# A gated mix of window attention and a feed-forward block, forward and backward: paired puts, first loads on two queues, a gate gradient summed on VectorE

## The chip, the cores and the metric

The kernel runs on one core of one Trainium2 chip. The metric is the device time of one execution in microseconds (us), lower being better, as the median of several executions. The engines are TensorE (PE, matmuls), VectorE (DVE), ScalarE (ACT), GpSimd (POOL) and SyncE (SP). DMAs are issued here from SP, ACT and POOL; an issue takes a place in the instruction stream of its engine, which is worked through in order.

## The reference

A gate mixes two branches over 2048 tokens of width 512, and the kernel returns the output together with the gradients of seven inputs.

```python
g = sigmoid((x * gate_w).sum(-1, keepdims=True))
# branch a: 32 heads of 16, causal, a window of 256 tokens
q, k, v = split(x @ wqkv);  p = softmax(mask(q k^T / 4));  a = (p v) @ wo
# branch b: gated ReGLU with 1376 hidden columns
gate = x @ W_gate;  up = x @ W_up;  gate = gate * (gate > 0);  b = (gate * up) @ W_down
# x is A_x in both branches
out = g * a + (1 - g) * b
out, vjp = jax.vjp(f, A_x, A_wqkv, A_wo, B_W_gate, B_W_up, B_W_down, gate_w);  grads = vjp(grad_out)
```

All arrays are bf16. The outputs are `out` and the gradients of `A_x`, `wqkv`, `wo`, the three feed-forward weights and `gate_w`.

## The kernel before

**An order that a planner writes.** The program is one long list of operations. Each has the engines that it may run on with an estimated cost in ns, the buffers it reads and writes, and a rank. `Flow.run` plays this list through with its own clock: whenever an engine is free, the ready operation of lowest rank is put on it, and its instructions are issued in that order. The order on each engine is thus fixed when the program is built. Costs of DMA issues are numbers in the calls (`ns=340` for a put, 430 or 1300 by default). `SEEDS` adds a small random part to the ranks of dense matmuls, 200 operations to a seed, so that another set of seeds gives another order. Where PE has nothing ready for long, the planner puts in a filling matmul.

**Buffers.** The on-chip arena is divided into rings, each with a number of places; an operation that opens a buffer waits, in the plan and on the chip, until the place is free. `KVT`, `QDT`, `KVr`, `K1r` and `dd` hold a stage's inputs, `R`, `OB`, `dkv` its results.

**The start.** `load_first` loads the first two halves of the x rows, the weights of the first head group, and the rows of the output's gradient, all from SP. The gate weights are loaded from POOL, once as a column (`gw_col`, spread over 128 columns as `gw_rep` by VectorE) and once for all partitions (`gw_b`). `rows_to_T` turns x and the gradient on PE, `proj` makes q, k, v and the gradient of the attention's result, and `gates` computes the gate.

**The attention.** 32 stages (8 groups of 4 heads, 4 blocks of 512 tokens) each run six units of scores from the queries' side (A) and six from the keys' side (N). Row products make scores (`L1003`), ScalarE takes the exponential (`L1045`), POOL masks (`L1021`), VectorE multiplies (`L1051`), and column products sum up (`L1071`). Between these, PE takes dense work: projections, the feed-forward block in 11 chunks (`front`, `back`), and weight gradients (`L672`, `L1354`). `load_stage` loads a stage's k, v, q from DRAM (`L950`, `L951`) and once more turned (`L952`, into `KVr`). `put` writes a stage's dq and O to `HD_d` in four pieces of 16 rows (`L933`), and `tasks_N` writes dk and dv (`L1155`). `dw` loads `HD_d` turned for the weight gradients (`L1257`), and `load_heads` loads it straight for the last part (`L1332`).

**The end.** `final` and `whole` make the output and the gradient of x, one tile of 128 tokens each. Each tile also gives one `dz` for every token. The gradient of `gate_w` is the sum over all tokens of dz times x: `gate_sum` makes it with one matmul for each of the 16 tiles (`L1421`), three tiles late, into one bank `dg`.

Of the kernel before, what the change touches and what calls it, by code (L numbers as in the profile page):

```python
# [30 lines left out]
def place(segs, dist):  # L31
# [21 lines left out]
    10644, 40677, 50928, 50391, 47256, 5130, 14352, 52294, 4187, 17826, 20428, 23758, 43565, 50024, 2925, 886,  # L53
    42283, 15231, 13752, 30525, 39203, 9215, 6352, 38931, 53278, 7326, 50008, 50973,
# [341 lines left out]
def kernel(  # L396
# [45 lines left out]
    HQ, OUTS, GLAG = (SP, ACTE), 2, 3  # L442
# [25 lines left out]
    nc.scalar.preload_act_table_set("natural_log_exp_and_others")  # L468
# [36 lines left out]
    nc.gpsimd.dma_start(gw_col[:], gate_w.rearrange("(c p) -> p c", p=P))  # L505
    nc.gpsimd.dma_start(gw_b[:], gate_w.partition_broadcast(P))
    nc.vector.tensor_copy(gw_rep[:], bc(gw_col[:], P))
# [24 lines left out]
    ring("QDT", 5, [P, W])  # L532
# [3 lines left out]
    ring("KVr", 4, [P, 4, P])  # L536
# [8 lines left out]
    ring("R", 3, [P, 4, P])  # L545
    ring("OB", 2, [P, W])
    ring("dkv", 3, [P, W])
# [16 lines left out]
    ring("rg", 4, [P, W])  # L564
# [30 lines left out]
    place_at["next"] = A0 + KB  # L595
    ring("wo4", 1, [P, DC, D], after=["QDT"])
    assert place_at["next"] <= rings["dd"].lo
    ring("wT3", 1, [P, 3 * DC, D], at=B0, after=["RW"])
    ring("RW3", 1, [P, NT, 4 * P], at=rings["dd"].lo, after=att)
# [5 lines left out]
    for nm, k in (("b_t", 3), ("x_t", 3), ("xs", 2)):  # L605
        ring(nm, k, [P, D], F32, after=att)
# [3 lines left out]
    ring("dz", 4, [P, 4], F32, after=att)  # L610
# [29 lines left out]
    def dma(fn, r=(), w=(), nbytes=0, rank=3, turn=False, deps=(), order=(), on=(SP,), ns=0, row=0):  # L640
        return op({e: 1000 if e == POOL else ns or (1300 if turn else 430) for e in on}, (lambda e: fn(EN[e])) if fn.__code__.co_argcount > len(fn.__defaults__ or ()) else (lambda e: fn()), r=r, w=w, 
                  nbytes=nbytes * (0.785 + 106 / (row or (256 if turn else 1024))), rank=rank,
                  deps=deps, order=order)
# [33 lines left out]
    by_pool = (POOL,)  # L677

    def load_proj(c):
        w3 = buf("w3")  # L680
        for w in range(3):
            dma(lambda q, w=w: q.dma_start(
                w3[:, :, w, :], A_wqkv[:, w * D + c * P:w * D + (c + 1) * P].rearrange("(c p) n -> p c n", p=P)),
                w=[(w3, w)], nbytes=128 * KB, rank=3, row=256, on=by_pool if c == 1 else (SP,))
# [4 lines left out]
    def load_ffn(fc):  # L689
        fs, f0 = fsz(fc), fc * P  # L690
        wg, wu, wdT = buf("wg"), buf("wu"), buf("wdT")
        for t_, src in ((wg, B_W_gate), (wu, B_W_up)):
            dma(lambda q, t_=t_, src=src: q.dma_start(t_[:, :, :fs], src[:, f0:f0 + fs].rearrange("(c p) f -> p c f", p=P)),
                w=[t_], nbytes=128 * KB, rank=3, row=256, on=by_pool if fc < 2 else (SP,))
# [9 lines left out]
    def load_first():  # L704
# [3 lines left out]
        def rows(dst, src_d, k):  # L708
            dma(lambda: nc.sync.dma_start(dst[:, 2 * k:2 * k + 2, :],
                                          src_d[2 * k * P:2 * (k + 1) * P, :].rearrange("(t p) d -> p t d", p=P)),  # L710
                w=[(dst, 0), (dst, ("half", k))], nbytes=256 * KB, rank=3)

        def weights(w):
            dma(lambda: nc.sync.dma_start(
                w3[:, :, w, :], A_wqkv[:, w * D:w * D + P].rearrange("(c p) n -> p c n", p=P)),
                w=[(w3, w)], nbytes=128 * KB, rank=3, row=256)
# [7 lines left out]
        dma(lambda: nc.sync.dma_start_transpose(out=woT[:], in_=A_wo[0:P, :]), w=[woT], nbytes=128 * KB, rank=3, turn=True)  # L724
        weights(0)
# [14 lines left out]
    load_first()  # L740
    for sb in range(1, NSB):
        load_rows(x_r, x_d, sb)
        load_rows(db_r, go_d, sb)
    load_ffn(0)

    def rows_to_T(dst, src, sb, rank):
        for h in range(2):
# [11 lines left out]
            for k in range(n):  # L759
# [3 lines left out]
                   r=[pt], w=[(dst, sb)], rank=1)  # L763

# [26 lines left out]
    def proj_weights(c, rank):  # L791
        w3, woT = wsets.pop(("p", c))
# [3 lines left out]
           r=[(w3, 1)], w=[(wi, 0)], rank=3)  # L796
        op({POOL: 1200}, lambda e: nc.gpsimd.tensor_copy(wi[:].rearrange("p c (h w d) -> p c w h d", w=2, d=Dh)[:, :, 1],
                                                         w3[:, :, 2, :].rearrange("p c (h d) -> p c h d", d=Dh)),
           r=[(w3, 2)], w=[(wi, 1)], rank=3)
# [741 lines left out]
```

## Time and profile before

| | |
|---|---|
| median of 3 runs | 836.26 us (834.75 to 839.38) |
| the profiled execution | 836.25 us |
| its span, first to last instruction | 834.5 us |
| mean granted TensorE clock | 0.994 |
| busy: PE, DVE, ACT, POOL | 817.0, 689.2, 603.8, 544.8 us |
| DMA moved | 152.17 MB |

The profile shows one execution. A row of a view by instructions gives the start and the time in us, the engine, the line of the kernel, the operation, the tile written and the tile read, and in square brackets how long the engine stood before and what ended that. "SPq" and "ACTq" are the queues' instruction streams, where DMA issues stand. A row by stretches gives, for every engine, the busy time and the number of instructions, then the granted clock, the share of the DMA engines and GB/s. A row by line gives counts and the least, median and greatest duration in ns.

### The profile page before, as it was taken

What the parts mean: (1) busy time and instruction counts of PE and PEld (TensorE: products, weight loads), DVE (VectorE), ACT (ScalarE), POOL (GpSimd) and SP (SyncE); (2) the same over time, 40 slices, a digit from 0 to 9 for tenths busy, and PEclk for the clock granted to TensorE, in tenths of its full rate; (3) what the DMA queues carried; (4) which work ended last, traced back from release to release, by engine and by line L of the source; (5) the groups of instructions that cost most, each with busy time, mean ns of one, the idle gap of its engine ahead of it and who ended that gap; (6) DMA issues with size and microseconds to landing.
All of it is one profiled execution on the core that took longest, in us unless ns stands there. A gap on an engine that the chain in (4) does not pass through costs nothing.

```text
span 834.5 us, 24001 instructions
## 1 busy us (share of the span) xinstructions
PE 817.0 (98%) x8717; PEld 368.9 (44%) x8717; DVE 689.2 (83%) x1264; ACT 603.8 (72%) x1223; POOL 544.8 (65%) x945
## 2 busy tenths in 40 slices
PE   8999999999999999899999989999999999999999
PEld 5533444445354445354444544343343343434444
DVE  3697899999999999799899878898899898934643
ACT  4877778788878878788888768878887887603222
POOL 5388668797697878779898445546655656401435
PEclk9999999999999999999999999999999999999999
DMA  8889647576678787889988895764686554497985
GB/s 226 224 188 204 142 117 182 109 186 166 117 200 165 160 199 170 201 208 182 227 194 182 213 218 166 185 166 115 180 192 182 160 171 126 92 308 198 280 220 173
DMA packets 317033, 152.17 MB, mean 182 GB/s; under 512 B 205233, under 2 KB 309234, under 8 KB 316274
## 3 DMA queue, kind: packets, MB, share of 16 engines
q1 hardware_dynamic: 298146, 136.22, 67.2%
q10 hardware_dynamic: 18192, 12.85, 5.2%
q0 software_dynamic: 576, 1.57, 0.8%
q8 instruction: 68, 1.11, 0.6%
q14 instruction: 51, 0.42, 0.2%
HBM read 55.02 MB, written 55.74 MB: 133 GB/s over the span
## 4 chain that ended last, share of the span: by engine, by line
PE 85%; DVE 5%; DMA 3%; POOL 2%; issue 2%; ACT 2%; SPq 1%; DVEq 0%; ACTq 0%; POOLq 0%
PE banks L672 38%; PE banks L1354 21%; PE banks L1003 14%; PE banks L1071 10%; DVE arena L1051 3%; POOL arena L1021 1%; ACT arena L1045 1%; POOL arena L878 1%; DMA ffn_d<-arena 1%; PE banks L1104 1%; PE banks L753 1%; DMA arena<-in_A_wqkv_dram 1%; DMA arena<-KV_d 1%; DMA KV_d<-arena 0%; PE banks L1421 0%
## 5 line engine op out<-in xcount | busy, mean ns | idle before, releaser
L1051 DVE TENSOR_TENSOR arena<-arena,banks 128x512 bf16<-128x512 bf16 (+2 forms) x768 | 461.8, 647 | 45.7 <-PE banks L1003 37.7
L1045 ACT ACTIVATE arena<-banks 128x512 bf16<-128x512 f32 (+2 forms) x768 | 398.7, 572 | 77.8 <-PE banks L1003 66.1
L1021 POOL TENSOR_SCALAR_AFFINE_SELECT arena<-arena 128x256 bf16<-128x256 bf16 (+1 forms) x736 | 350.0, 499 | 160.0 <-ACT arena L1045 138.7
L672 PE MATMUL banks<-arena 128*128 128x512 bf16 (+4 forms) x1984 | 394.9, 337 | 2.6 <-DMA arena<-in_A_wqkv_dram 2.1
L672 PEld LDWEIGHTS <-arena 128*128 128x128 bf16 (+1 forms) x1984 | 172.5, 99 | 156.8 <-issue 59.6
L1354 PE MATMUL banks<-arena 128*128 128x512 bf16 (+1 forms) x784 | 188.4, 381 | 1.2 <-DVE arena L1051 1.2
L1003 PE MATMUL banks<-arena 32*128 32x256 bf16 (+5 forms) x2816 | 162.4, 276 | 6.3 <-ACT arena L1045 3.0
L878 POOL TENSOR_TENSOR arena<-arena 128x512 bf16<-128x512 bf16 (+1 forms) x91 | 105.9, 1168 | 19.5 <-DVE arena L873 8.5
L1003 PEld LDWEIGHTS <-arena 16*128 16x128 bf16 (+1 forms) x2816 | 49.7, 92 | 155.4 <-issue 145.3
L650 ACT CAST arena<-banks 128x512 bf16<-128x512 f32 (+4 forms) x159 | 77.4, 497 | 50.9 <-PE banks L672 35.1
L1354 PEld LDWEIGHTS <-arena 128*128 128x128 bf16 (+1 forms) x784 | 69.2, 98 | 92.1 <-issue 21.1
L1071 PE MATMUL banks<-arena 128*32 128x384 bf16 (+5 forms) x2816 | 104.4, 278 | 3.4 <-POOL arena L1021 2.2
L1071 PEld LDWEIGHTS <-arena 128*32 128x32 bf16 (+1 forms) x2816 | 57.7, 94 | 42.0 <-issue 28.6
L1450 POOL TENSOR_TENSOR arena<-arena 128x512 bf16<-128x512 f32 x12 | 16.0, 1341 | 59.7 <-ACT arena L1449 27.9
L1100 POOL TENSOR_TENSOR arena<-arena 128x512 bf16<-128x512 f32 x32 | 37.0, 1157 | 17.5 <-issue 10.7
L1440 DVE SCALAR_TENSOR_TENSOR arena<-banks,g_all,arena 128x512 bf16<-128x512 f32 x12 | 8.9, 746 | 32.3 <-ACT arena L1449 19.7
L1449 ACT ACTIVATE arena<-banks,g_all 128x512 f32<-128x512 f32 x12 | 8.2, 687 | 32.4 <-DVE arena L1445 11.4
L878 DVE TENSOR_TENSOR arena<-arena 128x512 bf16<-128x512 bf16 (+1 forms) x41 | 28.4, 695 | 3.6 <-DMA ffn_d<-arena 3.5
L873 DVE SCALAR_TENSOR_TENSOR arena<-arena,banks 128x512 bf16<-128x512 bf16 (+1 forms) x44 | 29.8, 679 | 1.1 <-ACT arena L868 0.6
L868 ACT ACTIVATE arena<-banks 128x512 bf16<-128x512 f32 (+1 forms) x38 | 23.0, 604 | 4.2 <-PE banks L672 4.0
L652 DVE CAST arena<-banks 128x512 bf16<-128x512 f32 (+3 forms) x41 | 23.7, 589 | 2.5 <-PE banks L672 1.7
L1096 ACT ACTIVATE arena<-arena 128x512 f32<-128x512 f32 x32 | 20.2, 630 | 7.5 <-DVE arena L1095 7.4
(88 smaller groups left out, 412.6 us busy)
## 6 DMA issues: line engine op xcount, KB each, us to landing
ffn_d<-arena SPq DMA_DIRECT2D x40, 384.0 KB
arena<-ffn_d SPq DMA_DIRECT2D x88, 128.0 KB
out_dram<-arena SPq DMA_DIRECT2D x66, 128.0 KB
arena<-HD_d ACTq DMA_DIRECT2D x29, 256.0 KB
KV_d<-arena SPq DMA_DIRECT2D x32, 128.0 KB
QD_d<-arena SPq DMA_DIRECT2D x32, 128.0 KB
arena<-KV_d SPq DMA_DIRECT2D x32, 128.0 KB
arena<-QD_d SPq DMA_DIRECT2D x32, 128.0 KB
```

The lines of the kernel that those rows point to most:

```text
L650: nc.scalar.copy(out, in_)
L652: EN[e].tensor_copy(out, in_)
L672: return lambda start, stop: nc.tensor.matmul(out_fn(), lhsT=lhs_fn(), rhs=rhs_fn(), start=start, stop=stop)
L873: op({DVE: t_stt(W)}, lambda e, q=q, ups=ups: nc.vector.scalar_tensor_tensor(out=q["upm"][:fs, :], in0=q["rg"][:fs, :], scalar=0.0, in1=up ...
L878: op({POOL: t_pool(W, 2), DVE: DTT}, lambda e, q=q, k=k, a=a, b=b: EN[e].tensor_tensor(out=q["act"][:fs, k, :], in0=q[a][:fs, :], in1=q[b] ...
L1003: nc.tensor.matmul(bank, lhsT=lt[rs, ls], rhs=rt[rs, rsl], start=True, stop=True)
L1021: nc.gpsimd.affine_select(out=v.rearrange("p h (b k) -> p h b k", b=cnt), in_=v.rearrange("p h (b k) -> p h b k", b=cnt), compare_op=ALU.i ...
L1045: op({ACTE: t_act(w)}, lambda e, h=h: nc.scalar.activation(nxt.Pt[:, h, :w], nxt.S[h][:, :w], ACT.Exp), r=[nxt.S[h]], w=[(nxt.Pt, h)], rank=0)
L1051: op({DVE: t_dve(wc)}, lambda e, h=h: nc.vector.tensor_tensor(out=cur.Pd[:, h, :wc], in0=cur.Pt[:, h, :wc], in1=cur.dP[h][:, :wc], op=ALU. ...
L1071: nc.tensor.matmul(acc[32 * i:32 * i + wt.shape[1], q0:q0 + cnt * P], lhsT=wt, rhs=m[:, i % 2, col * P:(col + cnt) * P], start=(k == 0), s ...
L1100: op({POOL: t_pool(W, 2), DVE: t_dve(W)}, lambda e: EN[e].tensor_tensor(out=U[:], in0=ri[:], in1=qd[:], op=ALU.mult), r=[ri, qd], w=[U], r ...
L1354: nc.tensor.matmul(bank[:], lhsT=l_(), rhs=r_(), start=(lo + k == 0), stop=(lo + k == n - 1))
```

## The change

It has five parts.

1. dq and O are gathered for two token blocks in rings of `[P, 2, W]`, and `put` writes both at once after the odd block: 4 issues of 16 rows of 2 KB in place of 8 of 1 KB.
2. The first loads go out from SP and ACT alternately. The gate weights come in as four rows on ACT, are turned by one PE transpose and spread by VectorE; the copy for all partitions is loaded after the x rows. The activation table's load follows the DMA issues on ACT. The loads of the first feed-forward chunk and of the second head group, and the copies of the first group's weights, wait for later turns of x.
3. The gate gradient: 14 tiles are summed as dz times x in F32, the first on POOL, the others on VectorE; POOL splits the sum into two bf16 parts, and two matmuls with ones bring them into `dg`. The last two tiles are added by matmuls as before.
4. The rings `QDT`, `KVr`, `R`, `dkv`, `rg`, `b_t` and `x_t` get smaller.
5. The planner's costs of SP's issues are set anew, and there is a new set of `SEEDS`.

```diff
 SEEDS = (
-    10644, 40677, 50928, 50391, 47256, 5130, 14352, ...
+    49174, 34604, 21252, 10858, 43264, 6178, 26424, ...
-    HQ, OUTS, GLAG = (SP, ACTE), 2, 3
+    HQ, OUTS, DIRECT = (SP, ACTE), 2, 2
-    nc.scalar.preload_act_table_set("natural_log_exp_and_others")
-    nc.gpsimd.dma_start(gw_col[:], gate_w.rearrange("(c p) -> p c", p=P))
-    nc.gpsimd.dma_start(gw_b[:], gate_w.partition_broadcast(P))
-    nc.vector.tensor_copy(gw_rep[:], bc(gw_col[:], P))
-    ring("QDT", 5, [P, W])
+    ring("QDT", 3, [P, W])
-    ring("KVr", 4, [P, 4, P])
+    ring("KVr", 3, [P, 4, P])
-    ring("R", 3, [P, 4, P])
-    ring("OB", 2, [P, W])
-    ring("dkv", 3, [P, W])
+    ring("R", 2, [P, 4, P])
+    ring("OB", 2, [P, 2, W])
+    ring("dq", 2, [P, 2, W])
+    ring("dkv", 2, [P, W])
-    ring("rg", 4, [P, W])
+    ring("rg", 3, [P, W])
-    for nm, k in (("b_t", 3), ("x_t", 3), ("xs", 2)):
+    for nm, k in (("b_t", 2), ("x_t", 2), ("xs", 2), ("gx", 1)):
-        return op({e: 1000 if e == POOL else ns or (1300 if turn else 430) for e in on}, ...
+        return op({e: 1000 if e == POOL else ns or (1270 if turn else 470) for e in on}, ...
+    def load_gate():
+        dma(lambda q: q.dma_start(gw_4[:], gate_w.rearrange("(c p) -> c p", p=P)), w=[gw_in], ..., on=(ACTE,))
+        pt = buf("pro", [P, DC], BF)
+        op({PE: 60}, lambda e: nc.tensor.transpose(pt[:], gw_4[:], ident[:DC, :DC]), r=[gw_in], w=[pt], rank=0.1, mode="den")
+        def spread(e):
+            nc.vector.tensor_copy(gw_col[:], pt[:])
+            nc.vector.tensor_copy(gw_rep[:], bc(gw_col[:], P))
+        op({DVE: 500}, spread, r=[pt], w=[gw_out], rank=1)
-        rows(x_r, x_d, 0)
-        rows(x_r, x_d, 1)
-        weights(1)
-        weights(2)
-        rows(db_r, go_d, 0)
-        rows(db_r, go_d, 1)
...
-        weights(0)
+        rows(x_r, x_d, 0, SP)
+        rows(x_r, x_d, 1, ACTE)
+        weights(1, SP)
+        weights(2, ACTE)
+        weights(0, SP)
+        rows(db_r, go_d, 0, SP)
+        rows(db_r, go_d, 1, ACTE)
...
+    load_gate()
+    op({ACTE: 1300}, lambda e: nc.scalar.preload_act_table_set("natural_log_exp_and_others"), rank=4)
-    load_ffn(0)
...
+    load_ffn(0, [later[0]])
+    proj_weights(0, [later[2]])
+    load_gate_rows([later[3]])
...
     def put(src, c, half, sb, k, lane, kind):
+        if sb % 2 == 0:
+            return
         for g in range(4):
-            dma(lambda ...: nc.sync.dma_start(HD_d[c, k, r0:r0 + Dh, sb * W:(sb + 1) * W], src[lo:lo + Dh, :]),
-                r=[src], w=[(HD_d, (c, sb, kind))], nbytes=16 * KB, rank=3, ns=340)
+            dma(lambda ...: nc.sync.dma_start(HD_d[c, k, r0:r0 + Dh, (sb - 1) * W:(sb + 1) * W],
+                                              src[lo:lo + Dh].rearrange("p b s -> p (b s)")),
+                r=[src], w=[(HD_d, (c, sb - 1, kind)), (HD_d, (c, sb, kind))], nbytes=32 * KB, rank=3, ns=460, row=2048)
...
+    def gate_sum(t, dz, dz_bf):
+        done.append(t)
+        if len(done) > NT - DIRECT:
+            direct(lambda: dz_bf[:, 0:1], lambda: x_r[:, t, :], [dz_bf, x_r])
+            return
+        if len(done) == 1:
+            op({POOL: t_pool(W)}, lambda e: nc.gpsimd.tensor_scalar(gx[:], x_r[:, t, :], dz[:, 1:2], None, op0=ALU.mult), ...)
+        else:
+            op({DVE: t_stt(W)}, lambda e: nc.vector.scalar_tensor_tensor(
+                out=gx[:], in0=x_r[:, t, :], scalar=dz[:, 1:2], in1=gx[:], op0=ALU.mult, op1=ALU.add), ..., rank=4)
+        if len(done) == NT - DIRECT:
+            op({POOL: t_pool(W)}, lambda e: nc.gpsimd.tensor_copy(gx2[:, 0], gx[:]), ...)
+            op({POOL: t_pool(W, 2)}, lambda e: nc.gpsimd.tensor_tensor(out=gx2[:, 1], in0=gx[:], in1=gx2[:, 0], op=ALU.subtract), ...)
+            for k in range(2):
+                direct(lambda: ones_c[:], lambda k=k: gx2[:, k], [(gx2, k)])
```

Among the planner's costs, the turned loads of `L1257` go from 1900 to 2400 ns, those of the feed-forward activations (`L894`) from 1500 to 2000, and the loads of turned weights from 3200 to 2000 and 2200.

More of the change, by code (lines that the diff above doesn't have):

```diff
@@ L594 @@
     assert place_at["next"] <= B2, (place_at["next"], B2)
-    place_at["next"] = A0 + KB
-    ring("wo4", 1, [P, DC, D], after=["QDT"])
-    assert place_at["next"] <= rings["dd"].lo
     ring("wT3", 1, [P, 3 * DC, D], at=B0, after=["RW"])
-    ring("RW3", 1, [P, NT, 4 * P], at=rings["dd"].lo, after=att)
+    ring("wo4", 1, [P, DC, D], after=["RW"])
+    assert place_at["next"] <= B0 + 16 * KB
+    ring("RW3", 1, [P, NT, 4 * P], at=A0 + KB, after=att)
     assert place_at["next"] <= rings["PtA"].lo
@@ L763, in rows_to_T @@
                    r=[pt], w=[(dst, sb)], rank=1)
+        return turned
     def proj(c, which, sb, rank):
@@ L837, in gates @@
         accumulate(pz, [mm(lambda: pz[:], lambda c=c: gw_rep[:, c, :], lambda c=c: x_T[:, c, sl]) for c in range(DC)],
-                   [(x_T, sb)], 0.8 if sb else 1.6)
+                   [(x_T, sb), gw_out], 0.8 if sb else 1.6)
         op({ACTE: t_act(W)}, lambda e: nc.scalar.activation(ez_bc[:, sl], pz[:], ACT.Exp), r=[pz], w=[(ez_bc, sb)], rank=1)
-    proj_weights(0, 0.3)
+    wsets["pw", 0] = wsets.pop(("p", 0))
+    later = {}
     for sb in range(NSB):
-        rows_to_T(x_T, x_r, sb, 0.2)
+        later[sb] = rows_to_T(x_T, x_r, sb, 0.2)
         if sb:
@@ L1083, in tasks_A1 @@
         LO, de = (buf("acc") for _ in range(2))
-        ri, OB, U, pr, R = (buf(nm) for nm in ("ri", "OB", "U", "pr", "R"))
+        ri, U, pr, R = (buf(nm) for nm in ("ri", "U", "pr", "R"))
+        if sb % 2 == 0:
+            st["OB"] = buf("OB")
+        OB, half = st["OB"], sb % 2
         dd, qd = st["in", n][2], st["qd", n]
@@ L1114, in tasks_A2 @@
         c, half = divmod(hg, 2)
-        Da, dq = buf("acc"), buf("dkv")
+        Da = buf("acc")
+        if sb % 2 == 0:
+            st["dq"] = buf("dq")
+        dq, k = st["dq"], sb % 2
         def w2(a, i):
@@ L1158 @@
     for c in range(1, DC):
-        load_proj(c)
-        proj_weights(c, 3)
+        load_proj(c, [later[1]] if c == 1 else ())
+        proj_weights(c)
         for sb in range(NSB):
@@ L1166 @@
         if fc:
-            load_ffn(fc)
+            load_ffn(fc, [later[1]] if fc == 1 else ())
         front(fc)
@@ L1502 @@
             whole(t, late[t // 2], qks[t // 2])
-    while waiting:
-        emit_gate_sum([])
     dgs = buf("dgs", [1, D])
```

116 lines of the change are left out of this document (62 added, 54 removed).

## The prediction

> **What bounds the kernel now.** I read the page of the profile first, for the shares and the chain; then the busy time by stretches of 20 us, for where TensorE (PE) is not busy; then the chain of waits at those places, the order of time at both ends, and the DMA issues by line.
>
> ```profile
> span 834.5 us, 24001 instructions
> PE 817.0 (98%) x8717; PEld 368.9 (44%) x8717; DVE 689.2 (83%) x1264; ACT 603.8 (72%) x1223; POOL 544.8 (65%) x945
> ...
> PE 85%; DVE 5%; DMA 3%; POOL 2%; issue 2%; ACT 2%; SPq 1%; DVEq 0%; ACTq 0%; POOLq 0%
> ```
>
> PE is busy 98% of the span and carries 85% of the chain that ended last. The profiled execution took 836.25 us, 1.7 us of it outside the span, and the median of the three runs is 836.26, so I sum against 836.25. PE's work is nearly fixed, and what the change can win is PE's gaps, the two ends, and PE instructions that go away. The gaps are 834.5 - 817.0 = 17.5 us:
>
> ```profile
> core 0: us, PE busy (x) PEld busy (x) DVE busy (x) ACT busy (x) POOL busy (x), PEclk, DMA share, GB/s
> 0.00:20.00 20.00, 16.25 (x146) 10.55 (x147) 7.09 (x19) 8.45 (x17) 10.10 (x25) 0.91 0.81 226
> ...
> 60.00:80.00 20.00, 18.33 (x187) 7.18 (x184) 15.72 (x28) 14.34 (x29) 17.96 (x27) 1.00 0.90 191
> 80.00:100.00 20.00, 19.02 (x217) 8.95 (x215) 17.27 (x31) 15.71 (x31) 15.32 (x26) 1.00 0.83 174
> ...
> 340.00:360.00 20.00, 17.33 (x181) 7.23 (x179) 15.62 (x28) 14.49 (x29) 16.14 (x26) 1.00 1.06 264
> ...
> 480.00:500.00 20.00, 17.49 (x195) 8.41 (x199) 13.80 (x29) 11.84 (x24) 10.05 (x21) 0.92 0.93 211
> ...
> 540.00:560.00 20.00, 18.57 (x192) 7.37 (x190) 17.88 (x34) 15.61 (x36) 10.19 (x22) 0.91 0.73 183
> ...
> 720.00:740.00 20.00, 18.05 (x201) 7.54 (x194) 15.57 (x30) 6.70 (x16) 3.96 (x9) 1.00 0.68 199
> ...
> 800.00:820.00 20.00, 20.00 (x101) 9.52 (x100) 10.32 (x19) 4.85 (x11) 10.65 (x8) 1.00 0.92 266
> ```
>
> The first 20 us lack 3.75 us of PE. The six rows from 60 to 740 lack 1.67 + 0.98 + 2.67 + 2.51 + 1.43 + 1.95 = 11.2 us. In three of the rows the granted clock is also below 1: 0.08 and 0.09 of 20 us at 480 and 540 are 1.6 and 1.8 us more. So the start costs about 4 us, the middle about 14.6, and everything else is PE at work.
>
> **The start.** Here are both engines and the queues in order of time, then the DMA queues in the first 8.4 us:
>
> ```profile
> 0.81 1.28 ACT L468 ACT_TABLE_LOAD   x1 [0.81 <-PEq L1525]
> 0.82 0.98 SPq L709 DMA_DIRECT2D arena<-in_A_x_dram  x2
> ...
> 1.84 1.02 SPq L714 DMA_DIRECT2D arena<-in_A_wqkv_dram  x2
> ...
> 4.64 0.58 ACT L650 COPY arena<-banks 128x512 bf16<-128x512 bf16 x1 [2.54 <-PE banks L753]
> ...
> 5.50 0.83 PE L735 MATMUL banks<-ident 128*128 128x128 bf16 x12
> ...
> 6.53 0.43 DVE L507 COPY gw_rep<-gw_col 128x512 bf16<-128x512 bf16 x1 [1.45 <-DMA gw_col<-in_gate_w_dram]
> 6.88 0.75 DVE L652 COPY arena<-banks 128x512 bf16<-128x512 bf16 x2
> 8.40 3.33 PE L672 MATMUL banks<-arena 128*128 128x512 bf16 x8 [2.06 <-DMA arena<-in_A_wqkv_dram]
> 11.52 1.32 PE L672 MATMUL banks<-arena,gw_rep 128*128 128x512 bf16 x4
> ```
> ```profile
> q1 hardware_dynamic: 2212, 1.25, 52.3%
> q0 software_dynamic: 83, 0.15, 18.4%
> ```
>
> PE's first projection waits 2.06 us for wqkv. Three things stand ahead of that load. SP issues two x loads at about 0.49 us each, then two weight loads at 0.51. On the other queue, GpSimd's, the gate weights (a column gathered by single elements and a row for 128 partitions) and first weights take 18.4% of the DMA engines for 0.15 MB, against 52.3% for 1.25 MB: three times the engine time per byte. And VectorE stands 1.45 us on gw_col, with two copies of x_T queued behind it until 7.63.
>
> The change splits the issues over SP and ACT, so the second weight load leaves about two issues (1.0 us) earlier; it takes GpSimd's traffic out of this stretch and frees VectorE from gw_col. Ends: 0 and the 2.06 us of PE wait. I take 1.4, nearer the wait, since issue and traffic add up. What replaces it: the gate column arrives as four rows behind ACT's loads, and goes through one small PE transpose and a VectorE spread (0.43 us by L507). It is wanted only where the gw_rep matmuls stand (11.52), so I cost it at nothing; without that cover it costs up to the 1.45 us that VectorE waited. The table load (1.28) moves behind four ACT issues (about 2.0 us) and then ends near 4.1, ahead of ACT's first copy at 4.64: nothing. GpSimd's copies of wi and the loads of the first feed-forward chunk go later; nothing in the first 20 us reads them.
>
> The first eight projections take 3.33 us, 416 ns each, where four gw_rep matmuls take 1.32, 330 ns with their tail; the clock of the stretch is 0.91. 0.09 of 20 us is 1.8 us lost. PE had ended its twelve warming matmuls at 6.33 and then stood until 8.40. With the weights 1.4 us earlier that gap is under 0.7 us, and I expect the slow spell to go: 1.7 us, with 0 as the other end. The Trainium skill, "TensorE: Matmul & The Clock Gate", Part 1, says that the window which judges PE's activity runs freely and is not reset by a kernel's start; by that rule the spell could fall on other matmuls and the term is 0, so the sum 1.7 us higher. The rows at 480 and 540 agree that a gap brings a slow spell, while the row at 340, with a larger gap and clock 1.00, shows that it is not certain.
>
> The same skill, "DMA: Bandwidth & Descriptors", section "Issuing engines are not separate DMA queues", speaks against the two queues: all issuers end on the same engines, and a second one saves only issue time. By that rule alone the landing gain is the 1.0 us of issues and not 1.4.
>
> **Puts by pairs.** A put of dq or O leaves every second token block with 2 KB rows, so 256 issues on SP become 128.
>
> ```profile
> L933 SPq DMA_DIRECT2D HD_d<-arena x256: 315/418/1606, 75.4 to 740.8; - x128
> L1155 SPq DMA_DIRECT2D HD_d<-arena x32: 337/420/1227, 90.7 to 731.6; - x32
> ...
> L952 SPq DMA_TRANSPOSE arena<-KV_d x32: 1188/1224/1862, 18.2 to 656.2; - x32
> ```
>
> L1155 moves eight times the bytes of one L933 put with the same median, so a put of twice the bytes costs the same 0.42 us. SP loses 128 x 0.42 = 54 us out of the 665 us in which the puts lie. Everything queued on SP behind them (loads of the next stage, turned rows, activations) leaves earlier. The chain shows what that queue's lateness costs PE:
>
> ```profile
> 71.37 4.17 DMA KV_d<-arena
> ...
> 78.12 3.29 DMA ffn_d<-arena
> ...
> 339.53 3.44 DMA ffn_d<-arena
> ...
> 489.88 4.83 DMA arena<-KV_d
> ```
>
> These stand in the rows that lack 1.67, 0.98, 2.67 and 2.51 us, 7.8 in all, with 1.6 us of slow clock behind the last: 9.4 us. The new costs given to the planner for SP's issues, and the new seeds, give another order, which no row of before shows. So the ends are -9.4 (all gone) and +9.4 (as many new ones). I take a gain of a third, 3.1: SP is relieved by 54 of 665 us, which cannot remove waits on data that is really late, but shortens all of them. The put itself now comes one block later for even blocks. Its readers are the weight gradients and the head loads, which follow the attention; for the last head group the third block's rows come one stage, (734 - 30) / 32 = 22 us by the row products' ends below, later. PE works on from 734 to the tail's matmuls at 828.84 (below), some 95 us, so nothing is lost there.
>
> ```profile
> L1003 PE MATMUL banks<-arena x2816: 211/278/523, 29.7 to 734.2; 32*128 32x384 bf16 x39, 32*128 32x256 bf16 x33, 16*128 16x384 bf16 x30, 16*128 16x256 bf16 x29
> ```
>
> The rings that shrink to make room (QDT 5 to 3, KVr 4 to 3, R 3 to 2, dkv 3 to 2, rg 4 to 3, b_t and x_t 3 to 2) allow some loads only later. KVT, loaded and read beside QDT, already has three. KVr is the tight one; it is the slower rival below. I cost the rest at nothing, covered by PE's other work.
>
> **The gate's gradient.** Sixteen matmuls become four; the rest is summed on VectorE, and GpSimd splits the sum into two parts. The tail in order of time:
>
> ```profile
> 808.10 0.81 PE L1421 MATMUL banks<-arena 128*1 128x512 bf16 x3
> ...
> 828.84 2.97 PE L1421 MATMUL banks<-arena 128*1 128x512 bf16 x13
> ...
> 830.47 0.16 DVE L1482 CAST arena<-arena 128x1 bf16<-128x1 f32 x1
> ...
> 831.33 0.33 SPq L1492 DMA_DIRECT2D out_dram<-arena  x1
> ...
> 831.85 0.57 ACT L650 CAST arena<-banks 1x512 bf16<-1x512 f32 x1 [3.22 <-PE banks L1421]
> 832.45 0.26 SPq L1507 DMA_DIRECT2D out_dram<-arena  x1
> ```
>
> Twelve fewer at 2.97 / 13 = 0.23 us are 2.7 us of PE. But thirteen stood after the last product that the output needs, beside VectorE's own last steps. With two left there, the last dz is ready at 830.63, its matmul ends near 831.0, ACT's copy near 831.65, and the last DMA leaves after L1492 at 831.75 instead of 832.45: 0.7 us. Before the end three matmuls go and two of ones come: 0.2. I take 0.9; the ends are 0 and 2.7. The thirteen products on VectorE (0.75 us each by L1476 below, some 10 us) lie from 740 on, where it is busy 10.32 of 20 us. The three steps on GpSimd, about 1.3 us each at most by L1450, fit beside its 10.65.
>
> ```profile
> 828.95 0.75 DVE L1476 SCALAR_TENSOR_TENSOR arena<-banks,g_all,arena 128x512 bf16<-128x512 f32 x1 [6.93 <-PE banks L1354]
> ```
> ```profile
> L1450 POOL TENSOR_TENSOR arena<-arena 128x512 bf16<-128x512 f32 x12 | 16.0, 1341 | 59.7 <-ACT arena L1449 27.9
> ```
>
> **The sum.** 836.25 - 1.4 (landing) - 1.7 (clock) - 3.1 (stalls) - 0.9 (tail) = 829.15, say 829.2 us. About 0.5%, 4.2 us, is what a measurement of this kernel can tell from no change, so the bounds are 832.1 and 840.4.
>
> **The rivals.** *The middle does not move.* SP's relief is hidden, because PE always has dense work to take and its waits are set by the vector engines. For it: VectorE is busy 14 to 18 of 20 us in the rows with gaps. Against it: the four DMA pieces above. The time: 836.25 - 1.4 - 1.7 - 0.9 = 832.3, or 834.0 if the clock term fails too.
>
> *The new order closes most gaps.* The planner priced a put at 340 ns where the trace has a median of 418; with the costs of SP's issues set anew, an order may remove the four DMA stalls wholly and half of the other 1.43 + 1.95 + 1.8 = 5.2 us. The time: 836.25 - 4.0 - 9.4 - 2.6 = 820.2.
>
> *Slower: KVr with three places.* The turned load of KV (L952) may leave only when the sweep of three stages before is through, not four, so up to one stage of 22 us later. This is the very load that PE stood on at 489.88: 2.51 us, and 1.6 us of slow clock after it, 4.1 us a time. SP is in order, so whatever stands behind a waiting L952 waits too. It decides from the second such stall on, since two eat the 7.1 us won. With three more of them, and the relief of SP lost: 836.25 - 4.0 + 12.3 = 844.6. Against it: with four places it happened once in 32 stages, and a freed SP issues the load sooner.
>
> *The two queues do nothing* and the gate weights come too late for PE: no landing and no clock gain, and 1.45 us of wait moved onto PE: 836.25 - 3.1 - 0.9 + 1.45 = 833.7.
>
> **How the numbers follow.** The forecast has 0.53 of the chance, the closing of gaps 0.16, the unmoved middle 0.14, the two queues 0.07, the slower case 0.10. Faster by over 0.5% are the forecast but for 0.02, the closed gaps, and 0.05 of the unmoved middle (a little more tail gain, up to 2.7, is enough): 0.72. Slower is 0.10. The same is the rest, 0.18. The forecast's own range is 825 to 832. The range for 8 in 10 reaches down to 819, just past the closed gaps, and up to 836, past the unmoved middle and the idle queues; outside lie the slower case and the ends of the others.
>
> **What would show it.** Right: the first L672 near 7.0 us and its eight matmuls in about 2 us at clock 1.00; 128 puts with a median near 0.42 us; PE's lack between 60 and 740 us at 8 to 11 us; four matmuls for the gate gradient and the last DMA about 5 us after the last dense product. Wrong: a wqkv landing still after 8 us; puts at 0.8 us each; PE or GpSimd standing on KV_d loads in several stages; a tail in which PE waits for the sum on VectorE and GpSimd.

## The result, and the profile after

The changed kernel takes 827.9 us (median of four executions, 827.6 to 829.9), the kernel before 837.1 beside it (834.8 to 839.4). The ratio is 0.9895, with an interval of 0.9862 to 0.9928: faster by about 1%. The forecast was 829.2, but its parts did not come out as its total did.

The profiled execution took 829.9 us, the slowest of the four, while that of the kernel before, 836.25 us, lies in the middle of its own. So the traces show 6.3 us of the 9.2 between the medians. From the page of the changed kernel, the span and the busy times:

```profile
span 828.2 us, 23832 instructions
PE 810.4 (98%) x8704; PEld 366.3 (44%) x8704; DVE 700.6 (85%) x1278; ACT 607.1 (73%) x1226; POOL 546.9 (66%) x944
```

The span is 6.3 us shorter. The row products (L1003 before, L1029 now) cut it into three stretches: a start up to the first of them, the attention up to the last, and an end. From the view by line, these products and the puts of dq and O of the changed kernel:

```profile
L1029 PE MATMUL banks<-arena x2816: 211/278/498, 32.0 to 725.8; 32*128 32x384 bf16 x39, 16*128 16x384 bf16 x33, 32*128 32x256 bf16 x33, 16*128 16x256 bf16 x29
...
L958 SPq DMA_DIRECT2D HD_d<-arena x128: 314/420/2273, 74.2 to 736.9; - x128
```

| profiled execution of | span | start | attention | end |
|---|---|---|---|---|
| before | 834.5 | 29.7 | 704.5 | 100.3 |
| the changed kernel | 828.2 | 32.0 | 693.8 | 102.4 |

The start is 2.3 us longer, the attention 10.7 shorter, the end 2.1 longer: together the 6.3. All of the gain lies in the attention. There PE's gaps fall from 12.0 to 6.1 us, and about as many matmuls (7982 and 7993 records) are busy for 687.7 us instead of 692.5. At the end PE has 3.2 us less work and 5.3 us more gaps (7.0 instead of 1.7). There are 128 puts where there were 256, and one of twice the bytes takes the same 0.42 us.

The busy time by stretches of the changed kernel (length, then busy us and instructions of PE, PEld, DVE, ACT, POOL, then the granted clock, the DMA share and GB/s):

```profile
0.00:20.00 20.00, 16.29 (x149) 11.11 (x149) 9.28 (x24) 8.59 (x17) 7.45 (x22) 1.00 0.86 238
20.00:40.00 20.00, 19.05 (x173) 11.01 (x174) 10.56 (x24) 14.68 (x30) 7.72 (x16) 0.91 0.80 180
60.00:80.00 20.00, 19.51 (x220) 7.70 (x217) 18.78 (x32) 16.47 (x32) 17.89 (x27) 1.00 0.92 202
80.00:100.00 20.00, 18.55 (x220) 8.38 (x219) 18.85 (x33) 15.79 (x31) 14.97 (x25) 1.00 0.78 198
340.00:360.00 20.00, 20.00 (x269) 10.56 (x261) 19.75 (x34) 15.95 (x32) 17.64 (x29) 1.00 0.75 155
480.00:500.00 20.00, 20.00 (x242) 10.54 (x239) 15.52 (x32) 16.57 (x33) 14.03 (x29) 1.00 0.68 135
540.00:560.00 20.00, 18.86 (x216) 7.49 (x208) 18.27 (x32) 13.90 (x32) 10.43 (x23) 1.00 0.53 133
```

PE now lacks 0.49, 1.45, 0 and 0 us in the four stretches from 60, 80, 340 and 480 us where a DMA had been in the chain: 1.9 us instead of 7.8. The clock is 1.00 at 480 and 540, where it had been 0.92 and 0.91. The slow spell of the first 20 us has not gone, it stands in the next 20.

### The profile page after: what moved, and what is told of

It is laid out like the page before. It is cut to its first block, busy times and chain, and to the rows that moved or that the text cites. A ratio compares the mean times of both kernels' runs of the same rounds, so it can differ in the third digit from the quotient of the medians.

```text
span 828.2 us, 23832 instructions
## 1 busy us (share of the span) xinstructions
PE 810.4 (98%) x8704; PEld 366.3 (44%) x8704; DVE 700.6 (85%) x1278; ACT 607.1 (73%) x1226; POOL 546.9 (66%) x944
## 5 line engine op out<-in xcount | busy, mean ns | idle before, releaser
L1029 PE MATMUL banks<-arena 16*128 16x384 bf16 (+5 forms) x2816 | 160.3, 276 | 2.7 <-DVE arena L1127 1.1
L901 POOL TENSOR_TENSOR arena<-arena 128x512 bf16<-128x512 bf16 (+1 forms) x88 | 104.2, 1186 | 20.9 <-DVE arena L896 14.1
L1029 PEld LDWEIGHTS <-arena 16*128 16x128 bf16 (+1 forms) x2816 | 48.2, 92 | 147.9 <-issue 138.5
L650 ACT CAST arena<-banks 128x512 bf16<-128x512 f32 (+3 forms) x168 | 83.7, 509 | 35.8 <-PE banks L672 25.7
L1097 PE MATMUL banks<-arena 128*32 128x384 bf16 (+5 forms) x2816 | 102.6, 278 | 0.5 <-DVE arena L1077 0.2
L1493 POOL TENSOR_TENSOR arena<-arena 128x512 bf16<-128x512 f32 x12 | 15.7, 1306 | 48.8 <-DMA arena<-b_d 16.2
L1129 POOL TENSOR_TENSOR arena<-arena 128x512 bf16<-128x512 f32 x32 | 37.1, 1159 | 13.0 <-issue 8.5
L1496 ACT COPY arena<-banks 128x512 f32<-128x512 f32 x12 | 7.0, 584 | 40.4 <-POOL arena L1499 24.2
L901 DVE TENSOR_TENSOR arena<-arena 128x512 bf16<-128x512 bf16 (+1 forms) x44 | 30.2, 691 | 2.6 <-DMA ffn_d<-arena 1.9
L1499 POOL TENSOR_TENSOR arena<-arena 128x512 bf16<-128x512 f32 x12 | 16.0, 1339 | 15.8 <-DMA arena<-dx_p 8.4
L1127 DVE SCALAR_TENSOR_TENSOR arena<-banks,vec,arena 128x512 bf16<-128x512 f32 x32 | 23.8, 744 | 0.7 <-ACT arena L1126 0.4
```

The lines of the kernel that those rows point to most:

```text
L650: nc.scalar.copy(out, in_)
L901: op({POOL: t_pool(W, 2), DVE: DTT}, lambda e, q=q, k=k, a=a, b=b: EN[e].tensor_tensor(out=q["act"][:fs, k, :], in0=q[a][:fs, :], in1=q[b] ...
L1029: nc.tensor.matmul(bank, lhsT=lt[rs, ls], rhs=rt[rs, rsl], start=True, stop=True)
L1097: nc.tensor.matmul(acc[32 * i:32 * i + wt.shape[1], q0:q0 + cnt * P], lhsT=wt, rhs=m[:, i % 2, col * P:(col + cnt) * P], start=(k == 0), s ...
L1129: op({POOL: t_pool(W, 2), DVE: t_dve(W)}, lambda e: EN[e].tensor_tensor(out=U[:], in0=ri[:], in1=qd[:], op=ALU.mult), r=[ri, qd], w=[U], r ...
L1499: op({POOL: t_pool(W, 2)}, lambda e: nc.gpsimd.tensor_tensor(out=dx_sb[:], in0=xs[:], in1=x_t[:], op=ALU.add), r=[xs, x_t], w=[dx_sb], rank=1)
```

## The experiments

The theory was that SP's queue is the resource: fewer issues of puts let everything behind them leave earlier. The first rival was that the gain comes from another searched order; others were the longer rows as such, the start, and the gate's gradient. All ratios are to the kernel before, run on the same chip in the same set. Where a kernel keeps the order of another, every engine's instruction list stays as it was except for the issues named. A trace shows one execution; where several kernels share a start or an order, their traces show how far that varies.

**The pairs undone in the new order.** The plan stays, and each put of a pair is issued as two of one block each.

```diff
-  nc.sync.dma_start(HD_d[c, k, r0:r0 + Dh, (sb - 1) * W:(sb + 1) * W], src[lo:lo + Dh]...)
+  [nc.sync.dma_start(HD_d[c, k, r0:r0 + Dh, (sb - 1 + b) * W:(sb + b) * W], src[lo:lo + Dh, b]) for b in range(2)]
```

> The changed kernel with every instruction in its place, but each put of two blocks issued as two puts of one block (16 rows of 1 KB), both after the odd block: 256 issues on SP in place of 128. Theory A, SP's relief made the middle faster: about 54 us of issue come back on SP, the gaps between 40 and 730 us grow again by the 3.1 us that the prediction gave for it or more, 831 us or above. Theory B, the order made it: PE's stream is the same and the data still arrive in time, 828 us, within 1 us of the changed kernel.

Measured: 851.1 us, ratio 1.0104 [1.0059, 1.0149]. Against the changed kernel that is 1.0104 / 0.9895 = 1.021, some 17 us for 128 issues more. The two are from different sets; beside this run, on the same chip, the changed kernel with only its last additions altered (below) took 831.0 us. The rows are 1 KB again, too, so this run alone doesn't part issues from rows. The rows of this run by line, and then SP and those who waited, in order of time:

```profile
L958 SPq DMA_DIRECT2D HD_d<-arena x256: 314/418/2280, 75.2 to 757.5; - x128
...
L1029 PE MATMUL banks<-arena x2816: 211/278/523, 32.5 to 745.6; 32*128 32x384 bf16 x39, 16*128 16x384 bf16 x33, 32*128 32x256 bf16 x33, 16*128 16x256 bf16 x29
```
```profile
474.98 5.14 SPq L958 DMA_DIRECT2D HD_d<-arena  x8
480.16 0.97 SPq L1333 DMA_DIRECT2D arena<-ffn_d  x2
481.23 6.50 SPq L917 DMA_TRANSPOSE arena<-ffn_d  x3
...
494.88 0.53 SPq L976 DMA_DIRECT2D arena<-KV_d  x1
...
499.17 0.40 POOL L986 COPY arena<-arena 128x256 bf16<-128x256 bf16 x1 [4.18 <-DMA arena<-KV_d]
...
500.01 0.81 ACT L987 ACTIVATE arena<-arena,vec 128x512 bf16<-128x512 bf16 x1 [4.17 <-DMA arena<-KV_d]
...
501.36 0.58 PE L672 MATMUL banks<-arena 128*128 128x512 bf16 x1 [3.44 <-ACT arena L1071]
```

This is the path from an issue to a PE stall. SP works without a break from 475 us, eight puts of it 5.14 us; the load of the next stage's k and v (L976) comes to its turn at 494.88; POOL and ACT stand 4.2 us for it, and PE 3.44 us behind ACT. In the stretch after it the granted clock is 0.74:

```profile
500.00:520.00 20.00, 18.11 (x156) 7.68 (x162) 10.35 (x20) 13.64 (x27) 10.37 (x20) 0.74 0.28 70
```

That this kernel is slower even than the kernel before, which has as many puts, is not explained; its puts stand in bunches of eight behind every second block, in an order that was searched for half as many.

**One part of the change in the kernel before.** The order of every engine is kept. First O alone goes out by pairs (192 issues), then dq as well (128), from buffers that lie side by side, written in turn.

```diff
+  put_one = lambda ...: nc.sync.dma_start(HD_d[c, k, r0:r0 + Dh, (sb - 1) * W:(sb + 1) * W],
+      arena[lo:lo + Dh, <both blocks, side by side>]) if sb % 2 else None
-  dma(lambda ...: nc.sync.dma_start(HD_d[c, k, r0:r0 + Dh, sb * W:(sb + 1) * W], src[lo:lo + Dh, :]), ...
+  dma(lambda ...: put_one(src, c, k, sb, lo, r0, lane), ...
```

> The kernel before, every engine's order kept, only the puts of O done by pairs after the odd block (the even block's four issues are left out, the odd block's move 2 KB rows): 64 of the 256 put issues are gone from SP, nothing else. Splitting 128 puts again cost the changed kernel some 17 us. Theory A, SP's issue time is worth that much wherever it is taken away: 64 issues fewer give 4 to 8 us, a ratio to before of 0.990 to 0.995. Theory C, the order is only fitted to the issue times it was searched with, and a change of them in either direction is lost or worth nothing: within 1.5 us of before or above it.

> The kernel before, every engine's order kept, with the puts of both O and dq done by pairs after the odd block: 128 put issues in place of 256, all of part 1 of the change and nothing of the rest. dq's two blocks and dk/dv take fixed places of the ring that they shared. Taking away the first 64 issues gave 13 us (826.4 against 839.6). Theory A in a straight line: another 8 to 13 us, a ratio to before of 0.970 to 0.975. Theory A with an end to it (once SP keeps up, PE's work bounds): within 3 us of the kernel with O pairs alone, a ratio of 0.981 to 0.986.

Measured: O alone 826.4 us, 0.9843 [0.9812, 0.9874]; both 824.3 us, 0.9817 [0.9774, 0.9859]. So by these medians the pairs alone, in the old order, are worth more than the whole change. O alone gained 13 us where 4 to 8 had been expected at most. The first 64 issues taken out bring nearly all of it. Whether the second 64 add anything, these intervals can't say. The rows of the kernel with both, by line:

```profile
L930 SPq DMA_DIRECT2D HD_d<-arena x128: 314/418/1426, 84.9 to 730.6; - x128
...
L1003 PE MATMUL banks<-arena x2816: 211/277/332, 31.1 to 722.0; 32*128 32x384 bf16 x39, 32*128 32x256 bf16 x33, 16*128 16x384 bf16 x30, 32*128 32x128 bf16 x30
```

Its attention takes 690.9 us, 13.6 less than before, and its mean clock is 1.000. Who waited for the tile KV_d, which holds every stage's k and v in DRAM (us in total, times): in the kernel before, in this one, in the changed kernel, and in the changed kernel with the pairs undone.

```profile
  POOL arena L960: 11.3, 6
  ACT arena L961: 4.0, 1
  ACT arena L650: 1.8, 1
  DVE arena L960: 0.9, 1
  DVE arena L962: 0.4, 1
```
```profile
  POOL arena L1021: 1.1, 1
  POOL arena L960: 0.8, 2
  ACT arena L650: 0.8, 1
  DVE arena L960: 0.2, 1
```
```profile
  POOL arena L986: 2.9, 5
  ACT arena L987: 0.5, 1
  POOL arena L1047: 0.3, 1
  PEld L672: 0.2, 1
  DVE arena L986: 0.2, 1
```
```profile
  POOL arena L986: 13.1, 9
  ACT arena L987: 5.8, 2
  DVE arena L986: 1.1, 2
  DVE arena L988: 0.6, 1
...
```

18.4, 2.9, 4.1 and 21.0 us in all. In these four traces the waits on a stage's inputs fall by some four fifths with the pairs, and come back without them. In three more traces of the changed kernel's attention with paired puts (the runs of the one queue, the gate's gradient and the last additions below) they are 9.1, 8.4 and 4.3 us, while the attention takes 692.9, 694.0 and 692.7. So the fall is by half or more, and the sum of these waits is a sign of SP's lateness but no measure of the time. Busy time of the stretch from 40 to 722 us in the kernel before, with both pairs, and changed:

```profile
40.00:722.00 682.00, 671.07 (x7777) 297.55 (x7777) 616.92 (x1105) 550.09 (x1110) 491.42 (x874) 0.99 0.73 173
```
```profile
40.00:722.00 682.00, 677.08 (x7919) 300.88 (x7917) 628.88 (x1126) 557.52 (x1127) 495.83 (x884) 1.00 0.74 175
```
```profile
40.00:722.00 682.00, 676.14 (x7886) 299.39 (x7888) 626.03 (x1120) 559.54 (x1129) 497.10 (x881) 1.00 0.75 177
```

PE lacks 10.9, 4.9 and 5.9 us there. Over the whole of its attention, with the same matmuls, the kernel with both pairs has 7.1 us less of gaps than before (12.0 to 4.9) and 6.5 us less of busy PE (692.5 to 686.0). The clock, 0.99 against 1.00, goes with the second part; the slow stretches at 480 and 540 us account for 3.4 us of it, and the rest is not located.

**Issues or longer rows?** The kernel with both pairs, but each put of 16 rows issued as two of 8: the same rows of 2 KB, the same bytes, 256 issues again.

```diff
-  put_one = lambda ...: nc.sync.dma_start(HD_d[c, k, r0:r0 + Dh, ...], arena[lo:lo + Dh, ...]) if sb % 2 else None
+  put_one = lambda ...: [nc.sync.dma_start(HD_d[c, k, r0 + 8 * h:r0 + 8 * h + 8, ...],
+                                           arena[lo + 8 * h:lo + 8 * h + 8, ...]) for h in range(2)] if sb % 2 else None
```

> The kernel before with both puts by pairs, in which each put of 16 rows of 2 KB is issued as two of 8 rows of 2 KB: 256 issues on SP again, the same bytes, rows and packets as with 128. Pairs alone gave 824.3 us against 839.3. If SP's issue time is what the pairs save, the gain is lost: 836 us or more, a ratio to before of 0.995 or above. If the longer rows (half the packets of the puts) are what they save, it stays: 824 to 827 us, a ratio of 0.980 to 0.986.

Measured: 830.1 us, 0.9919 [0.9881, 0.9956], against 0.9817 [0.9774, 0.9859] with whole puts. Its puts by line:

```profile
L930 SPq DMA_DIRECT2D HD_d<-arena x256: 276/294/1752, 84.6 to 736.6; - x128
```

A put of 8 rows takes 0.29 us. Count times median gives 107 us of puts before, 54 by pairs, and 75 here: 40% of the issue time that was saved is back, and 1.0 of the 1.8% of gain is lost. Neither of the two times expected came; the result lies between them. So the issues matter with the rows held equal, for about half of the gain; the two kernels ran on different chips, but each against the kernel before beside it. Whether the other half is issue time as well or the longer rows stays open, and so does whether a half-sized put lands as soon as a whole one: the profiled execution, 826.8 us, was one of the faster of nine (824.9 to 835.3) and shows no stalls (3.0 us on KV_d) that would explain the median.

The pairs take one more thing off SP. Before, a put of O can come to its turn on SP when VectorE's last step for it (L1098) is not done, and SP stands with all that is behind it. Without the even block's put this mostly goes. The kernel before, and with both pairs:

```profile
SPq L933 <- DVE arena L1098: 16.1, 6, 5.1
```
```profile
SPq L930 <- DVE arena L1098: 3.1, 1, 3.1
```

These 13 us happen to be the size of the gain, but they don't lie where PE stands: in the kernel before, SP stands 1.8 to 5.2 us ahead of puts at 133, 217, 571, 671 and 691 us, and PE is busy for 20.00 of 20 us in each of those stretches. In the changed kernel no put waits for O's step for more than 0.2 us in all, and splitting its puts adds next to none of this but costs 17 us. So this waiting is at most a part; no run takes it away alone.

**More off SP.** The changed kernel with the 32 puts of dk and dv issued from ACT; the order is otherwise kept.

```diff
-  dma(lambda: nc.sync.dma_start(HD_d[c, 2 + half, :, sb * W:(sb + 1) * W], o[:]),
+  dma(lambda: nc.scalar.dma_start(HD_d[c, 2 + half, :, sb * W:(sb + 1) * W], o[:]),
```

> The changed kernel with the 32 puts of dk and dv (128 KB each) issued from ScalarE in place of SP, at the same places of the planned order; PE, VectorE and GpSimd keep their order. SP loses 18 us of issue, ScalarE gains some 14. Theory A: 1 to 3 us faster than the changed kernel, a ratio to before near 0.986. Theory C: 2 us or more slower, since ScalarE's exponentials, which feed the row products, wait behind the puts.

Measured: 831.3 us, 0.9915 [0.9882, 0.9947]: no gain over the changed kernel; neither the 1 to 3 us less nor the 2 us more that were expected. Another 32 x 0.44 = 14 us off SP (the median of these puts in the changed kernel) are worth nothing here; on ACT they take 0.34 us each, 11 us. Either SP's lateness no longer decides, as the small second step of the pairs suggests too, or ACT pays as much; this run doesn't tell which.

**The searched orders.** Only `SEEDS` differ: each kernel with the other's, and both with the same arbitrary ones.

```diff
 SEEDS = (
-    49174, 34604, 21252, 10858, ...
+    10644, 40677, 50928, 50391, ...    (the other kernel's; or 21223, 9887, 25876, 42660, ... in both)
```

> The changed kernel with the seeds of before, so another order of the dense work with all structural parts kept. Theory A (parts, not order): 828 us, within 2 us. Theory B (the searched order carries most of the gain): 834 us or more.

> The kernel before with the seeds of the changed one. Those seeds were not searched for its list of operations, so this shows what an unsearched order costs the kernel before. Theory A: 837 us, within 2 us. Theory B: 840 to 846 us, about as far above before as the changed kernel with old seeds is above itself.

> The changed kernel with a third, arbitrary set of seeds. With the seeds of before it took 863 us. If that is what an unsearched order costs this kernel, again 855 to 868 us; if those seeds were unlucky, 828 to 845 us.

> The kernel before with the same arbitrary seeds that gave the changed kernel 838.2 us. If unsearched orders cost both kernels alike, 850 to 866 us, as the other unsearched order of before (863); if the changed kernel's parts make it less sensitive to its order, this one stands above 838 by more than the 9 us between the two searched kernels.

| seeds | kernel before | changed kernel |
|---|---|---|
| of before | 1 | 1.0270 [1.0227, 1.0313] |
| of after | 1.0242 [1.0190, 1.0294] | 0.9895 [0.9862, 0.9928] |
| arbitrary | 1.0235 [1.0185, 1.0285] | 0.9966 [0.9937, 0.9995] |

The kernel before loses 2.4% with either of the two other sets, more than was expected of the first. The changed kernel loses 3.8% with the old seeds but only 0.7% with the arbitrary ones, so how much a set that was not searched costs can't be told beforehand. With the same seeds in both, the changed kernel is slower by 2.7%, or faster by 3.4% or 2.6%. One draw is worth more than the whole change, so the total of two searched kernels can't be divided into parts by drawing again. That is why the runs that keep the order carry the argument.

**The start on one queue.** All first loads of the changed kernel are issued from SP, in the same order otherwise.

```diff
-  dma(lambda q: q.dma_start(dst[:, 2 * k:2 * k + 2, :], ...      # x and gradient rows, and the weights alike
+  dma(lambda q: nc.sync.dma_start(dst[:, 2 * k:2 * k + 2, :], ...
```

> The changed kernel with its first loads all issued from SP, at the same places of the order: three of them move from ScalarE's queue to SP's. The prediction gave 1.0 us to the issues. If two queues start the loads earlier, PE's first projection moves from 7.9 to about 9 us and the time rises by 1 us or less; if all queues share the same engines and the later rows set the pace, the time stays within 0.5 us; a cascade through the fitted order, as with the split puts, would give several us.

Measured: ratio 0.9882 [0.9847, 0.9918], no difference from 0.9895. But the traces differ at the start. First the changed kernel in order of time, then this one:

```profile
4.52 1.04 PE L771 MATMUL banks<-ident,arena 128*128 128x128 bf16 x8 [1.06 <-DMA arena<-in_A_x_dram]
...
7.91 1.27 PE L672 MATMUL banks<-arena 128*128 128x512 bf16 x4
...
20.57 0.23 PE L771 MATMUL banks<-ident,arena 128*128 128x128 bf16 x1 [1.64 <-DVE arena L846]
```
```profile
3.83 1.03 PE L771 MATMUL banks<-ident,arena 128*128 128x128 bf16 x8 [0.36 <-DMA arena<-in_A_x_dram]
...
6.44 1.46 PE L672 MATMUL banks<-arena 128*128 128x512 bf16 x6
```

On one queue the x rows are there 0.7 us sooner and the first projection begins 1.5 us sooner, where 9 us had been expected; the first row product stands at 28.7 us instead of 32.0. This trace is of the fastest execution of its kernel, 826.4 us where the median is 830.8. But five traces of the start on two queues all have x at 4.52 to 5.02 us, the first projection at 7.91 to 8.29 and the first row product at 32.0 to 32.5, so the difference at the start is not chance. With two queues the first weights leave 0.5 us after the first x rows, with one 1.0 us. That x and the weights then share the DMA engines, so that the load that everyone needs first lands later, is the likely reason; no run shows it by itself. Why the two ratios hardly differ even so is not shown.

**The gate's gradient.** The changed kernel with sixteen matmuls as before in place of the sum on VectorE. The planner's order stays the same up to the last part, and differs from there.

```diff
-    gx, gx2 = buf("gx"), buf("gx2")
...
+        wsets["dg"] = op({PE: t_mm(1)}, lambda e: nc.tensor.matmul(dg[:], lhsT=dz_bf[:, 0:1], rhs=x_r[:, t, :], start=first, stop=end), ...
```

> The changed kernel with the gate's gradient summed by sixteen matmuls as before; the order is the same up to the last part. The prediction gave this part 0.9 us, so 1 us slower than the changed kernel, a ratio to before near 0.990 to 0.991. If the tail of the changed kernel is set by GpSimd's adds and its two extra steps there, no difference or up to 1 us faster.

Measured: 834.1 us, 0.9953 [0.9926, 0.9980], 0.6% above the changed kernel. Its attention takes 694.0 us, the same; the end takes 109.6 instead of 102.4. In order of time, the largest wait there:

```profile
752.89 11.10 PE L1386 MATMUL banks<-arena 128*128 128x512 bf16 x43 [2.78 <-DMA arena<-HD_d]
```

PE stands for a load of `HD_d`, which the gate's gradient doesn't read. So the 0.6% is at least in part that of another order of the end: twelve matmuls at 0.23 us would be 2.7 us, and the end is 7.2 longer. (The profiled execution, 837.6 us, is 3.5 above the median.) What the sum on VectorE is worth alone stays open.

**The last additions.** In the changed kernel the last addition of dx may run on VectorE too; again only the order of the last part differs.

```diff
-  op({POOL: t_pool(W, 2)}, lambda e: nc.gpsimd.tensor_tensor(out=dx_sb[:], in0=xs[:], in1=x_t[:], op=ALU.add),
+  op({POOL: t_pool(W, 2), DVE: DTT}, lambda e: EN[e].tensor_tensor(out=dx_sb[:], in0=xs[:], in1=x_t[:], op=ALU.add),
```

> The changed kernel, with the last add of the tiles done in two parts (the gradient of x) allowed on VectorE as well as on GpSimd; the order is the same up to the last part. In the changed kernel dense work ends near 821 us of 828.2 and GpSimd's adds run on to 824.3. If GpSimd's adds set the end, the tail shortens by 1.5 to 2.5 us, 826 us. If the late loads of the partial sums set it, nothing changes, 828 us.

Measured: 831.0 us, 0.9876 [0.9846, 0.9906], no difference from the changed kernel. GpSimd's additions stand last at the end (below), but a planner free to move them, which puts seven of the twelve on VectorE, gains nothing that can be measured; an addition for the output (L1493), which was not free, is GpSimd's last there.

**The fastest version** is the kernel before with both pairs and its old order: 824.3 us, with an interval that ends at 0.9859, where that of the changed kernel begins at 0.9862. The two are from different sets, so their order is likely rather than shown. In the profiled executions the changed kernel is 5.8 us longer: 0.9 at the start, 2.9 in the attention, 2.0 at the end. So nothing here shows a gain of the other four parts together.

## Why the prediction was right, and where not

The total was right by luck: the middle brought more than was forecast, and the start and the end lost what was forecast as their gain. Term by term, in the profiled execution:

- **Stalls in the middle: -3.1 forecast, -10.7 measured.** The mechanism was right: half the puts at an unchanged 0.42 us each, and the loads behind them earlier. The term that was mis-sized is this one, by "a gain of a third". In three of the four stretches where the chain had named a DMA the lack of PE went or shrank, in the fourth it grew by 0.5 us (together 7.8 to 1.9 us), and the slow spells at 480 and 540 went too. The reason given, that relief of SP "cannot remove waits on data that is really late", failed: with the pairs in the old order, three of the six gaps from 60 to 740 us (340, 480 and 540) are gone, and both slow spells. The measured size lies at the end of the stated bounds, -9.4, and a little beyond.
- **Landing of the first weights: -1.4 forecast, -0.5 measured**: the first projection begins at 7.91 instead of 8.40 us, where 7.0 was forecast. Such a pair of executions is little: four traces with the old start have 8.40, 8.55, 9.75 and 9.78 us, five with the new 7.91 to 8.29, so on average it is about 1.0 us. The step that failed is the split over two queues, put down as a gain; on one queue it is 6.44, so the rest of the change brings 2 us or more and the second queue takes about 1.5 back. The Trainium skill, "DMA: Bandwidth & Descriptors", section "Issuing engines are not separate DMA queues", had all issuers end on the same engines; these traces are in line with it.
- **Slow clock at the start: -1.7 forecast, nothing gained.** Clock 1.00 in the first 20 us, 0.91 in the next, and so in all five traces with the new start. The step that failed is that closing the gap ahead of the first projection ends the slow spell. In three of four traces with the old start the first 20 us have 0.91; in the fourth, with both pairs, the clock is 1.00 throughout the first 40 us, though PE stood 2.48 us there. In the new start PE stands 1.64 us for VectorE near 20.57 us, but the trace of the one queue has the same stand at 18.90 and no slow spell. So no one gap decides. The first row product came at 32.0 to 32.5 us, where the old start has 29.7 to 31.1. The Trainium skill, "TensorE: Matmul & The Clock Gate", Part 1, has a window that runs freely; a spell that moves or stays away is in line with that.
- **The tail: -0.9 forecast, +2.1 measured** over the whole end. The end of the changed kernel in order of time:

```profile
821.16 0.59 PE L1465 MATMUL banks<-arena,ones_c 128*1 128x512 bf16 x2
...
821.59 0.59 PE L1465 MATMUL banks<-arena 128*1 128x512 bf16 x2
...
822.22 0.57 ACT L650 CAST arena<-banks 1x512 bf16<-1x512 f32 x1 [0.33 <-PE banks L1465]
823.02 1.26 POOL L1499 TENSOR_TENSOR arena<-arena 128x512 bf16<-128x512 f32 x1
...
824.31 0.33 SPq L1501 DMA_DIRECT2D out_dram<-arena  x1
824.74 0.54 SPq L1314 DMA_DIRECT2D out_dram<-arena  x1
825.37 0.43 SPq L1548 DMA_DIRECT2D out_dram<-arena  x1
```

The gate's gradient is indeed four matmuls, and ACT has its copy done at 822.8. But its store (L1548) is still the last issue, 2.6 us later, because SP works in order: the store of dx (L1501) stands ahead and leaves when GpSimd's last addition ends at 824.3. That is what the forecast did not look at. From the end of the dense products to the end of the span it is 7.0 us where it had been 5.6. This is an account of the end as a whole, which has another order too; what the gate's sum alone brings stays open, as said.

Of the rivals, the closing of most gaps was right for the middle, and wrong in laying it on the new order: the old order with pairs does the same. The two idle queues were half right. The KVr rival did not come: PE has no wait on a KV_d load worth more than 0.2 us. The unmoved middle is refuted by the attention, 10.7 us shorter, and by the runs with and without pairs.

## What to carry to other kernels

A queue that issues DMAs in order is an engine that the busy shares leave out: count its issues, multiply by their median, and ask whose input stands behind them, before judging a small transfer to be free. To find what one part of a change to a planned kernel is worth, change what an operation issues and keep the order; a new search moves the time by more than the part does. And when several stalls of a chain have the same late queue behind them, weigh the case that relieving it removes them all: here it did for most of them, and a third was far too little.

## What the runs showed of the hardware

- An issue's time did not go by bytes: on SP, 16 rows of 1 KB and 16 rows of 2 KB have a median of 0.42 us, 128 rows of 1 KB 0.40 to 0.44, 8 rows of 2 KB 0.29.
- The first 64 issues taken off SP, 27 us of its time by the median, moved the end by 13 us (0.9843 of 839.6), though SP is in none of the busy shares. What the next 64 moved is too small to tell.
- With two queues for the first loads PE had the first x rows at 4.52 to 5.02 us in five traces, with one at 3.83 (and at 3.57 to 3.71 in four traces of the old start), so later and not sooner.
- A slow spell at the start is not the same in every execution of one order: 0.91 in three traces of the first 20 us, 1.00 in a fourth.
